# RWKV-7 attention and a hard-swish feed-forward on one core: conversion's steps dealt by a table, and two groups of loads issued later

## The chip, the core and the metric

The kernel runs on one NeuronCore of one Trainium2 chip. The metric is the device time of one launch in microseconds (us); the time before is the median of three runs.

## The reference

Two blocks follow each other. The first is a linear-attention recurrence over 768 steps for 4 batches and 8 heads of 40 features. The second takes its result as 3072 tokens of 320 features through a feed-forward with 2048 hidden features.

```python
for t in range(S):
    y[:, :, t] = einsum('bhd,bhde->bhe', rt, state)
    Sa = einsum('bhde,bhe->bhd', state, at)
    state_decay = state * wt[:, :, None, :] - einsum('bhd,bhe->bhde', Sa, bt)
    state = state_decay + einsum('bhd,bhe->bhde', vt, kt)
x = attn_out.transpose(0, 2, 1, 3).reshape(3072, 320)
h = x @ w_in
out = (h * clip(h + 3, 0, 6) / 6) @ w_out
```

## The kernel before, in words

**Units and groups.** The recurrence is cut in blocks of 64 steps. A unit is one block of two batches (two times 64 steps on the 128 partitions) with all eight heads; there are 24 units, in groups of NU = 4. A unit is first prepared (`prepare`): stage W (turn w, running products), gam (decay factors), A, B and K (turn a, b, k and scale them), F (the 64x64 coupling of a and b), factor (scaled K and B in row form, `KBt`), E (masked scores) and EV (scores times v). Then the triangular coupling of the whole group is inverted (`invert`: 30 pairs of a product and an addition, L661 and L667, one after the other on VectorE), completed by `third_block` (L697 to L730), and each unit takes its step (`step`: RT, VT, C, R, S, U, UT, rS, sn, H, y, then `move` and `move2`, which carry the result to the feed-forward's layout by DMA).

**Feed-forward.** `expand` (L975, with ScalarE L990 and VectorE L991 behind it) and `contract` (L1016) work on tiles of 128 tokens. After the first group they fill the tensor engine beside the later units.

**Conversion of the weights.** The two feed-forward weights arrive as raw 64-bit words and are turned into 32-bit floats in 20 pieces (`load_weights`). A piece of 512 KB is loaded by one to four DMAs (L279) into a temporary home and then takes VectorE's L301, ScalarE's L302 and L304, and VectorE's L321, L325 and L312. `load_weights` is a generator: every `next(weights)` issues one step of it. A home is loaded again only after the piece that was in it is done, and never beyond `limit`.

**What sets the order.** There is no scheduler: every engine and every queue works in the order in which the program emits instructions. The SyncE queue (SP) issues nearly all DMAs, each in its place in that order. Around the change this order has four stretches:

1. `by_twos(0, ...)` prepares units 0 to 3 in turns t = 0 to 13. `fetch` is called inside stages: W fetches the next W, A the next A, factor the next B and K. In `gam_stage` (L503) a unit up to 8 fetches its own v. At t == 0 the first `next(weights)` loads the first two pieces into `tinv` (four DMAs); `limit` then goes to 4 at t == 7 and to 12 at t == 10.
2. `while not third` emits the inversion of the first group. Every third turn, and at a small rate in `by_twos` (MIXED), a step of conversion is put in.
3. `PLAN` emits the steps of units 0 to 3 and the two `third_block` calls (`firsts`, written T). The argument `weight` of `run` puts conversion steps after each pause of a stage: none or 1 in `firsts`, 1.5 on average up to line 6 of the plan, 3 from line 7.
4. At line 8 of the plan the W and A tiles of the second group are allocated and loaded (`seconds`, tile WA). From line 10 the second group's preparation is mixed in, and from there the kernel runs in its steady form.

Of the kernel before, what the change touches and what calls it, by code (L numbers as in the profile page):

```python
# [30 lines left out]
def kernel(  # L31
# [43 lines left out]
    B, H, T, D = r.shape  # L75
# [3 lines left out]
    NU = 2 * NP  # L79
# [107 lines left out]
    for i in range(3):  # L187
        t = const.tile([P, H, BL], F32, name=f"score{i}")
# [14 lines left out]
    for p in range(NP):  # L203
        t = const.tile([P, 2, NPR, SLOT], F32, name=f"state{p}")
        nc.vector.memset(t[:], 0.0)
        state.append(t)
        t = const.tile([P, 2, NPR], F32, name=f"last{p}")
# [175 lines left out]
    def fetch(name, i, engine=None):  # L383

        if i is None or i >= NK:
            return
        x, crossed = {"W": (w, 0), "A": (a, 0), "B": (b, 0), "K": (k, 0), "R": (r, 1),
                      "V": (v, 1)}[name]
        if name == "V":
            t = values[i % AHEAD]  # L390
        else:
            t = (others if i < 2 * NU and i % 2 and name != "R" else inputs)[name]
        g, p = names[i]
        engines = engine or nc.sync
        for q in range(2):
            engine = engines[q] if isinstance(engines, tuple) else engines
            y = x[2 * p + q, :, g * BL:(g + 1) * BL, :]
            rows = slice(q * BL, (q + 1) * BL)
            if crossed:
                for s in range(2):  # L400
                    engine.dma_start(out=t[rows, 4 * s:4 * s + 4, 0:D],  # L401
                                     in_=y[s::2].rearrange("h t e -> t h e"))
            else:
                engine.dma_start(out=t[rows, :, 0:D], in_=y.rearrange("h t e -> t h e"))  # L404
        data[i][name + "N"] = t
# [8 lines left out]
    def turn_pairs(x):  # L414

        o = ps_any([P, NPR, P])
        for n in range(NPR):
            nc.tensor.transpose(out=o[:, n, :],  # L418
                                in_=x[:, 2 * n:2 * n + 2, :].rearrange("p s e -> p (s e)"),
                                identity=ident[:])  # L420
        return o
# [21 lines left out]
    def turned(name):  # L443
        return tmp.tile([P, NPR, P], F32, name=name, tag="turned", bufs=5)
# [24 lines left out]
    def prepare(i, F):  # L469
        n, o = i % NU, data[i]  # L470
# [19 lines left out]
        def gam_stage():  # L490

            gam = o["G"] = grp.tile([P, NPR, P], F32, name="gam", tag="gam", bufs=NU + 2)
            rgam = o["rg"] = tmp.tile([P, NPR, P], F32, name="rgam", bufs=2)
            gv = gam[:].rearrange("p r (q i) -> p (r q) i", q=2)
            rv = rgam[:].rearrange("p r (q i) -> p (r q) i", q=2)
            nc.vector.reciprocal(gv[:, :, 0:HB], o["prods"][:, :, 0, 1:HB + 1][:, :, ::-1])  # L496
            nc.gpsimd.tensor_copy(gv[:, :, HB:BL], o["prods"][:, :, 1, 0:HB])
            nc.gpsimd.tensor_copy(rv[:, :, 0:HB], o["prods"][:, :, 0, 0:HB][:, :, ::-1])
            dec = grp.tile([P, 2, 2, NPR], F32, name="dec", tag="dec", bufs=NU + 2)
            nc.gpsimd.tensor_copy(dec[:].rearrange("p m q r -> p r q m"),  # L500
                                  o["prods"][:].rearrange("p (r q) m i -> p r q m i", q=2)[:, :, :, :, HB])
            o["dec"] = dec
            if i <= 2 * NU:  # L503
                fetch("V", i)
            yield from ()

# [93 lines left out]
        def k_stage():  # L600
            x = turn_pairs(o["KN"])
            yield PE
            kt = o["kt"] = turned("kt")
            nc.vector.tensor_tensor(out=kt[:], in0=x[:], in1=o["rg"][:], op=ALU.mult)

# [24 lines left out]
    def in_turn(stages, order):  # L630

        for name in order:
            yield from stages[name]()
            shared[0] = None
            yield DONE
# [410 lines left out]
    weights = load_weights()  # L1046
    side = deque()
    owed, due = [0.0], [0.0]
# [9 lines left out]
    def aside(n, weight=0):  # L1058

        for _ in range(n):  # L1060
            if side and next(side[0], side) is side:
                side.popleft()
            due[0] += weight
            while due[0] >= 1:
                due[0] -= 1
                next(weights, None)

    def run(stage, steps=0, weight=0, mixed=0):

        for at in stage:  # L1070
            if at == DONE:
                return
            aside(steps, mixed)
            due[0] += weight
            while due[0] >= 1:
                due[0] -= 1
                next(weights, None)

    third, F, group_F = [], None, []

# [11 lines left out]
    RFETCH, EARLY, MIXED = 8, 5, 0.27  # L1092
    TWOS = 14

    def by_twos(first, steps, mixed, rate, fill={}):


        chains = [by_stages(first + i, prepared(first + i)) for i in range(NU)]
        for t in range(TWOS):

            order = [0, 1] if t < STAGES else []
            order += [2, 3] if t > 5 else []
            if t < 2:
                order = [0, 0, 1, 1][4 * t:]
            if t == 3:
                order = [2, 0, 3, 1]
            for i in order:
                run(chains[i], steps if t > 10 else 0, fill.get(t, 0), mixed)
                pieces(rate / 2)
            if t == 10:  # L1110
                side.append(invert(group_F[-1], third, first == 0))
            yield
# [5 lines left out]
        for i in range(2):  # L1118
            fetch(name, i, (nc.sync, nc.scalar) if name == "W" else None)
    for t, _ in enumerate(by_twos(0, 4, MIXED, 0)):  # L1120
        if t == 0:
            next(weights)
        limit[0] = {7: 4, 10: 12}.get(t, limit[0])
        while t == 7 and refill[0]():
            pass
        if t == RFETCH:
            fetch("R", 0)
# [5 lines left out]
    stages = [step(i) for i in range(NU)]  # L1133
    chains = [in_turn(stages[0], ["RT", "VT", "C", "R"]), in_turn(stages[1], ["RT", "VT", "C"])]
    early = deque(chains[i] for i in (0, 0, 1, 1, 0, 1, 0))
    n, cleared = 0, []
    while not third:
        aside(1)
        if not third:
            n += 1  # L1140
            if n % 3 == 1:
                next(weights, None)
            if converted[0] >= 2 and not cleared:
                cleared.append(nc.gpsimd.memset(tinv[:], 0.0))
            if n % EARLY == 0 and early:
                run(early.popleft())
    assert not early and cleared
    limit[0] = 13
    while phase[0] == 1:
        next(weights)  # L1150
    firsts = [third_block(*third[-1], n, True) for n in (0, 2)]
    run(firsts[0])
    run(firsts[0], weight=1)

    def block(i, j):

        if i % NU < 2:
            if j == 0:
# [3 lines left out]

    PLAN = """0 U 0 UT 1 R
              0 sn 0 H T
              1 U 1 UT 0 y
              2 RT T
              1 sn 1 H 2 VT 0 move 0 move2
              1 y 2 R  # L1170
              2 S 3 RT
              1 move 1 move2 2 U 2 UT 2 C
              3 R 3 VT
              2 rS 2 sn 2 H 3 S
              2 y 3 U 3 UT 3 C
              3 rS 3 sn 3 H 2 move
              3 y 2 move2

              3 move
              3 move2"""  # L1180
    PLAN = [deque(line.split()) for line in PLAN.split("\n")]
    BEGIN = 10
    order = [[] for _ in range(NU)]
    plan = []
    for line in PLAN:
        plan.append([])
        while line:
            i = line.popleft()
            if i != "T":
                i = int(i)  # L1190
                order[i].append(line.popleft())
            plan[-1].append(i)
    chains = [in_turn(stages[i], order[i]) for i in range(NU)]
    for t, line in enumerate(plan):
        for i in line:
            if i == "T":
                run(firsts[1])
            else:
                run(chains[i], weight=1.5 if t < 7 else 3)
        if t == 3:  # L1200
            limit[0] = PIECES
        if t == BEGIN - 2:
            seconds()
            for name in "WA":
                fetch(name, NU + 1)
            third.clear()
            second_group = by_twos(NU, 3, 0, 1.25)
        if t == BEGIN + 1:

            for name in "BK":  # L1210
                others[name] = second(name)
                fetch(name, NU + 1)
        if t >= BEGIN - 2:
            pieces(3 if t < BEGIN else 1.5 if t < BEGIN + 3 else 0)
        if t >= BEGIN:
            next(second_group)
# [93 lines left out]
    for i in range(NU, NK):  # L1310
        spread[0] = i >= 2 * NU - 1
        for j in range(BLOCKS):
            rate, inversion = 3.5, 0
            if i + AHEAD >= NK + NU - 1:
                rate = 4.5
            if i < 2 * NU - 1:
                rate = 2.8
            parts = a_block(m)
            next(parts)
            if side or i % NU == NU - 1 and rate < 4:  # L1320

                rate, inversion = 6.2, 2 + (i < 2 * NU)
# [7 lines left out]
            if side:  # L1330
                rate, inversion = 6.2, 2 + (i < 2 * NU)
# [39 lines left out]
```

## Time and profile before

| | |
|---|---|
| median of 3 runs | 824.27 us (823.3 to 826.4) |
| the profiled execution's own time | 823.12 us |
| its span, first to last instruction | 821.4 us |
| granted tensor clock, mean over the span | 0.948 |
| PE busy | 742.0 us, 90% of the span |
| PE busy in 0 to 140 us | 82 us of 140 (sum of the ten-us windows) |
| PE busy in 140 to 820 us | 660.36 us of 680 |
| VectorE (DVE) busy | 534.1 us, 65% |
| ScalarE (ACT) busy | 321.5 us, 39% |
| GpSimd (POOL) busy | 152.4 us, 19% |
| moved by DMA | 45.05 MB, of it 2.05 MB on queue q8 (instructions) |

A timeline line has the start and the length in us, the engine, the source line, the operation, what it writes and reads, how many instructions are merged, and in brackets how long the engine stood idle before it and what ended that. The word "issue" stands where no wait is visible. In the groups of DMA queues, the columns are packets, MB and the share of 16 engines' time.

### The profile page before, as it was taken

How to read it: one execution, taken by the hardware profiler on the slowest of the kernel's cores; microseconds unless marked ns; L12 is line 12 of the kernel's file. 1: busy time of each engine (PE TensorE's matmuls, PEld its weight loads, DVE VectorE, ACT ScalarE, POOL GpSimd, SP SyncE). 2: the span in 40 equal slices, each digit the busy share in tenths (PEclk: the TensorE clock that was granted, in tenths of full speed). 3: DMA queues.
4: the chain of work that ended last, by engine and by line, in shares of the span. 5: the costliest groups of instructions: out<-in, count | busy, mean ns of one | idle time of the engine just before them, and what ended most of it. 6: DMA issues, size and time to landing. Idle time of an engine off the chain costs nothing.

```text
span 821.4 us, 35781 instructions
## 1 busy us (share of the span) xinstructions
PE 742.0 (90%) x15832; PEld 630.1 (77%) x15832; DVE 534.1 (65%) x1090; ACT 321.5 (39%) x847; POOL 152.4 (19%) x297
## 2 busy tenths in 40 slices
PE   4723976989999989999999999999999999999998
PEld 3622866878877878788888888878888888888886
DVE  7799598778855679735699564798546685232210
ACT  1233664222455423544333644334552434332211
POOL 3232101320122130321121222113112102000000
PEclk9855589998999999999999999999999999999999
DMA  6673544331223330332231232132232101110000
GB/s 100 121 181 78 138 119 90 66 59 26 41 50 61 57 63 14 59 53 48 46 59 24 53 66 49 36 57 38 42 61 51 18 22 29 28 21 13 18 19 16
DMA packets 174218, 45.05 MB, mean 55 GB/s; under 512 B 157424, under 2 KB 172784, under 8 KB 174064
## 3 DMA queue, kind: packets, MB, share of 16 engines
q1 hardware_dynamic: 171840, 42.36, 26.8%
q8 instruction: 125, 2.05, 1.0%
q10 hardware_dynamic: 2224, 0.41, 0.3%
q14 instruction: 29, 0.24, 0.1%
HBM read 34.08 MB, written 3.93 MB: 46 GB/s over the span
## 4 chain that ended last, share of the span: by engine, by line
PE 72%; DVE 9%; issue 9%; SPq 3%; DMA 3%; POOL 2%; ACT 2%; DVEq 0%; POOLq 0%; ACTq 0%
PE h L975 24%; PE o L1016 22%; PE any L456 4%; PE any L890 3%; PE any L418 3%; PE any L428 2%; PE any L866 2%; PE any L810 2%; DVE x L667 1%; SPq L401 1%; PE any L771 1%; DVE prod L661 1%; PE any L831 1%; SPq L404 1%; PE any L697 1%
## 5 line engine op out<-in xcount | busy, mean ns | idle before, releaser
L975 PE MATMUL h<-xt,win 128*128 128x128 f32 (+1 forms) x2304 | 251.4, 283 | 9.1 <-DVE gt L991 7.9
L975 PEld LDWEIGHTS h<-xt,win 128*128 128x128 f32 (+1 forms) x2304 | 231.6, 192 | 26.3 <-issue 8.9
L1016 PE MATMUL o<-wout,gt 128*128 128x320 f32 x768 | 230.8, 444 | 0.0
L1016 PEld LDWEIGHTS o<-wout,gt 128*128 128x128 f32 x768 | 138.6, 190 | 50.5 <-issue 0.4
L991 DVE SCALAR_TENSOR_TENSOR gt<-gt,h 128x512 f32<-128x512 f32 x96 | 61.5, 677 | 60.9 <-ACT gt L990 60.9
L990 ACT ACTIVATE gt<-h,three 128x512 f32<-128x512 f32 x96 | 62.2, 686 | 97.5 <-PE h L975 97.2
L875 DVE TENSOR_TENSOR state<-any,state 40x160 f32<-40x160 f32 (+1 forms) x88 | 27.9, 321 | 68.1 <-PE any L866 41.8
L661 DVE TENSOR_TENSOR prod<-x 128x30 f32<-128x30 f32 (+9 forms) x180 | 62.8, 349 | 13.8 <-POOL x L652 8.4
L905 POOL TENSOR_TENSOR yg<-ys,gam 128x512 f32<-128x512 f32 x22 | 39.4, 1789 | 165.7 <-DVE ys L903 110.5
L667 DVE TENSOR_TENSOR x<-x,prod 128x30 f32<-128x30 f32 (+9 forms) x180 | 64.1, 356 | 5.4
L591 POOL TENSOR_TENSOR KBt<-K,rgt 128x320 f32<-128x320 f32 x24 | 21.2, 884 | 246.9 <-ACT rgt L581 225.5
L465 DVE COPY_PREDICATED score<-mask,any 128x256 f32<-128x256 int32 x143 | 53.4, 435 | 6.1 <-PE h L456 3.0
L496 DVE RECIPROCAL gam<-prods 128x256 f32<-128x256 f32 x24 | 41.8, 1748 | 13.6 <-POOL yg L905 13.2
L624 ACT ACTIVATE EV<-any 64x160 f32<-64x160 f32 x92 | 24.8, 296 | 44.3 <-PE any L618 34.8
L511 DVE RECIPROCAL rgam<-prods 128x256 f32<-128x256 f32 x24 | 41.8, 1741 | 0.0
L903 DVE TENSOR_TENSOR ys<-any,ys 128x256 f32<-128x256 f32 x44 | 16.6, 418 | 34.6 <-PE any L618 18.3
L485 DVE TENSOR_TENSOR_SCAN prods<-wm,start 128x528 f32<-128x528 f32 x24 | 30.0, 1251 | 10.7 <-ACT wm L482 8.4
L750 ACT ACTIVATE RT<-any 128x256 f32<-128x256 f32 (+1 forms) x44 | 15.5, 401 | 51.5 <-PE any L428 49.5
L890 PE MATMUL any<-score,KBt 64*64 64x64 f32 x1536 | 31.1, 231 | 1.7 <-DVE state L875 1.7
L890 PEld LDWEIGHTS any<-score,KBt 64*64 64x64 f32 x1536 | 27.3, 144 | 4.5 <-DVE state L875 1.8
L730 ACT ACTIVATE tinv<-any 32x256 f32<-32x256 f32 x48 | 18.0, 375 | 30.3 <-PE any L720 29.7
L776 DVE TENSOR_TENSOR RR<-any,EV 128x160 f32<-128x160 f32 x44 | 12.1, 318 | 25.9 <-PE any L456 25.8
(181 smaller groups left out, 1057.0 us busy)
## 6 DMA issues: line engine op xcount, KB each, us to landing
B<-in_b_dram SPq DMA_DIRECT2D x48, 80.0 KB
K<-in_k_dram SPq DMA_DIRECT2D x48, 80.0 KB
V<-in_v_dram SPq DMA_DIRECT2D x96, 40.0 KB
out_dram<-ob SPq DMA_DIRECT2D x47, 80.0 KB
R<-in_r_dram SPq DMA_DIRECT2D x92, 40.0 KB
A<-in_a_dram SPq DMA_DIRECT2D x40, 80.0 KB
W<-in_w_dram SPq DMA_DIRECT2D x39, 80.0 KB
xt<-yg SPq DMA_DIRECT2D x72, 40.0 KB
```

Source lines behind the costliest of these rows:

```text
L456: nc.tensor.matmul(out=o[i][half(q), n, :], lhsT=lhs[half(i, D), n ^ (2 * q * swap), half(q)], rhs=rhs[half(i, D), n, half(q)], start=True ...
L465: nc.vector.copy_predicated(out=x[:, 4 * i:4 * i + 4, :], mask=mask4, data=o[i])
L496: nc.vector.reciprocal(gv[:, :, 0:HB], o["prods"][:, :, 0, 1:HB + 1][:, :, ::-1])
L511: nc.vector.reciprocal(rv[:, :, HB:BL], o["prods"][:, :, 1, 1:HB + 1])
L661: nc.vector.tensor_tensor(out=pv, in0=_ap(x[:], (i + 1) * L + i, [[L, n], [0, i]]), in1=_ap(x[:], i * L, [[0, n], [1, i]]), op=ALU.mult,)
L667: nc.vector.tensor_tensor(out=rest, in0=rest, in1=pv, op=ALU.add)
L890: nc.tensor.matmul(out=y[q][half(s), pr, :], lhsT=o[name][half(q), h * D:h * D + SLOT], rhs=m[name][half(q), 4 * rs + 2 * s + j, :], start ...
L905: nc.gpsimd.tensor_tensor(out=yg[:], in0=m["ys"][:].rearrange("p r q t -> p r (q t)"), in1=o["G"][:], op=ALU.mult)
L975: nc.tensor.matmul(out=hp[c][:, i, :], lhsT=lhsT, rhs=rhs, start=(begun[c] == 0), stop=(begun[c] == 3 * NQ - 1))
L990: nc.scalar.activation(out=gt[:], in_=hp[c][:], func=AF.Relu, bias=three[:], scale=1.0)
L991: nc.vector.scalar_tensor_tensor(out=gt[:], in0=gt[:], scalar=6.0, in1=hp[c][:], op0=ALU.min, op1=ALU.mult)
L1016: nc.tensor.matmul(out=op[:], lhsT=gts[c][:, n, :], rhs=wout[:, c * HJ + r * NQ + n, :], start=((split or r == 0) and c == 0 and n == 0), ...
```

## The change

Three things are edited.

- **v later.** Units 0 to 3 fetch their v in `k_stage` and no longer in `gam_stage`. Units 4 to 8 fetch theirs where they did.
- **First raw pieces later.** The first `next(weights)` is called at t == 5 and no longer at t == 0.
- **Conversion by a table.** In the inversion a step is put in at the turns listed in `STEPS`. In the plan, `name:n` puts n steps after every pause of that stage; X and Y are the two `third_block` calls. The stages themselves keep their order.

```diff
@@ gam_stage
-            if i <= 2 * NU:
+            if NU <= i <= 2 * NU:
                 fetch("V", i)
@@ k_stage
             yield PE
+            if i < NU:
+                fetch("V", i)
@@
+    def deal(n):
+        for _ in range(n):
+            next(weights, None)
+
-    def run(stage, steps=0, weight=0, mixed=0):
+    def run(stage, steps=0, mixed=0, deals=0):
         for at in stage:
             if at == DONE:
                 return
             aside(steps, mixed)
-            due[0] += weight
-            while due[0] >= 1:
-                due[0] -= 1
-                next(weights, None)
+            deal(deals)
@@ first group
-        if t == 0:
+        if t == 5:
             next(weights)
@@ inversion
+    STEPS = (1, 4, 7, 9, 12, 16, 17, 22, 27, 28, 32, 33, 34, 41, 44, 46, 51, 61, 64)
-            if n % 3 == 1:
+            if n in STEPS:
                 next(weights, None)
@@ plan
-    run(firsts[0])
-    run(firsts[0], weight=1)
-    PLAN = """0 U 0 UT 1 R
-              0 sn 0 H T
-              1 U 1 UT 0 y
-              2 RT T
-              1 sn 1 H 2 VT 0 move 0 move2
-              1 y 2 R
-              2 S 3 RT
-              1 move 1 move2 2 U 2 UT 2 C
-              3 R 3 VT
-              2 rS 2 sn 2 H 3 S
...
+    PLAN = """X X 0U:3 0UT:1 1R
+              0sn:1 0H:2 Y:1
+              1U 1UT:3 0y:2
+              2RT:2 Y
+              1sn 1H:1 2VT:1 0move 0move2
+              1y:2 2R
+              2S:1 3RT
+              1move 1move2 2U:3 2UT:2 2C:4
+              3R:4 3VT:3
+              2rS:3 2sn:3 2H:3 3S:3
...
-                run(chains[i], weight=1.5 if t < 7 else 3)
+            run(chains[name[0]], 0, 0, *map(int, amounts))
```

More of the change, by code (lines that the diff above doesn't have):

```diff
@@ L1093, with by_twos @@
     TWOS = 14
-    def by_twos(first, steps, mixed, rate, fill={}):
+    def by_twos(first, steps, mixed, rate):
         chains = [by_stages(first + i, prepared(first + i)) for i in range(NU)]
@@ L1107, in by_twos @@
             for i in order:
-                run(chains[i], steps if t > 10 else 0, fill.get(t, 0), mixed)
+                run(chains[i], steps if t > 10 else 0, mixed)
                 pieces(rate / 2)
@@ L1161, in block @@
             run(blocks[i])
-    PLAN = """0 U 0 UT 1 R
-              0 sn 0 H T
-              1 U 1 UT 0 y
-              2 RT T
-              1 sn 1 H 2 VT 0 move 0 move2
-              1 y 2 R
-              2 S 3 RT
-              1 move 1 move2 2 U 2 UT 2 C
-              3 R 3 VT
-              2 rS 2 sn 2 H 3 S
[L1175 to L1181, printed above, removed]
-    BEGIN = 10
[L1183 to L1193, printed above, removed]
-    for t, line in enumerate(plan):
[L1195 to L1198, printed above, removed]
-                run(chains[i], weight=1.5 if t < 7 else 3)
+    PLAN = """X X 0U:3 0UT:1 1R
[8 more added lines that the diff above has]
+              2rS:3 2sn:3 2H:3 3S:3
+              2y:3 3U:4 3UT:2 3C:5
+              3rS:3 3sn:3 3H:3 2move
+              3y:1 2move2
+              3move
+              3move2"""
+    BEGIN = 10
+    plan = [[x.split(":") for x in line.split()] for line in PLAN.split("\n")]
+    chains = {str(i): in_turn(stages[i], [x[0][1:] for line in plan for x in line if x[0][0] == str(i)])
+              for i in range(NU)}
+    chains.update({x: firsts[n] for n, x in enumerate("XY")})
+    for t, line in enumerate(plan):
+        for name, *amounts in line:
+            run(chains[name[0]], 0, 0, *map(int, amounts))
         if t == 3:
```

## The prediction

> **What bounds the kernel now.** I read the page's forty slices first, then the chain that ended last, then the timelines of SP, PE, DVE and ACT for the first 150 us, and last the DMA queues in one-us windows. From 140 us PE is busy 660.36 of 680 us in an order that the change leaves alone, so the end is set by when the dense part begins. In the first 140 us it is busy about 82. So a microsecond won before 140 moves the end by about one.
>
> The start is a queue of DMA issues. SP's timeline:
>
> ```profile
> 10.53 1.27 SPq L404 DMA_DIRECT2D W<-in_w_dram  x2
> 11.84 2.61 SPq L401 DMA_DIRECT2D V<-in_v_dram  x4
> 14.55 1.27 SPq L404 DMA_DIRECT2D WA<-in_w_dram  x2
> 15.87 2.62 SPq L401 DMA_DIRECT2D V<-in_v_dram  x4
> 18.53 2.00 SPq L279 DMA_DIRECT2D tinv<-in_moe_w_in_dram  x4
> 20.63 1.29 SPq L404 DMA_DIRECT2D A<-in_a_dram  x2
> ```
>
> SP issues without a pause, 0.65 us for each DMA, and unit 3's w (WA) stands behind unit 0's v. PE and DVE show who waits:
>
> ```profile
> 18.26 1.09 PE L418 MATMUL h<-ident,WA 128*128 128x128 f32 x4 [2.17 <-DMA WA<-in_w_dram]
> 29.14 0.36 PE L456 MATMUL any<-at,kt 40*64 40x64 f32 x1 [3.38 <-issue]
> 20.13 1.26 DVE L485 TENSOR_TENSOR_SCAN prods<-wm,start 128x528 f32<-128x528 f32 x1 [1.94 <-issue]
> 30.10 0.44 DVE L465 COPY_PREDICATED score<-mask,any 128x256 f32<-128x256 int32 x1 [3.04 <-PE h L456]
> ```
>
> From 30.10 DVE works on with no idle before the transpose that opens the inversion but 1.09 us (38.74), and from 42.28 to 77 it is full. The second stall, in the midst of unit 1's scores E, has no visible releaser. The DMA queues in the windows 23 to 24 and 26 to 27 us show one:
>
> ```profile
> q1 hardware_dynamic: 73, 0.24, 100.9%
> q8 instruction: 1, 0.02, 9.4%
> ```
>
> The raw weights fill all 16 engines[...]. The other place that matters lies later:
>
> ```profile
> 122.12 0.43 DVE L301 TENSOR_SCALAR parts<-raw_fb 128x512 uint32<-128x512 uint32 x1 [0.46 <-DMA raw_fb<-in_moe_w_out_dram]
> 124.44 1.26 ACT L990 ACTIVATE gt<-h,three 128x512 f32<-128x512 f32 x2
> 125.89 2.08 PE L975 MATMUL h<-xt,win 128*128 128x128 f32 x8 [4.30 <-DVE gt L991]
> 143.94 1.49 PE L890 MATMUL any<-score,KBt 64*64 64x64 f32 x62 [1.66 <-DVE state L875]
> ```
>
> PE waits for gt, gt for ACT's conversion steps ahead of it (122.58 to 124.06), these for piece 17's load. The last line is the hand-over: DVE, full from 130 to 145, releases PE into the dense part.
>
> [...] q8 has 125 packets in 2.05 MB. PE stalls at about its 216th matmul and again at about the 466th (1.17 us before 40.37)[...]. The trace has clock 0.50 from 44 to 102 us and again around 110 to 114.
>
> **The change, part by part** (times in the frame of the trace before).
>
> *v and raw pieces leave the front of SP.* Four DMAs go from ahead of unit 3's w: it is issued at 11.84, 2.7 us earlier. Unit 2's w took 2.3 us from the end of its issue to PE's start, so unit 3's is there at about 15.5, before PE has finished B at 15.9. PE loses its 2.17 us wait and shifts by 2.36. DVE's second scan then waits only for ACT's copies, which wait for the scan before (ends 17.60): 18.45 in place of 20.13, a gain of 1.7; unit 0's mask ends at 25.4.
>
> *The refill.* [...] In flight then are v, W and A, no raw piece: SP reaches those only after B and K of units 2 and 3, whose tiles GpSimd frees at 22.8 and 24.5, so B and K go from 22.8 to 28.0 and the raw pieces at 28.0. [...] PE goes on at 25.2, its scores end at 26.15. DVE's mask moves from 30.10 to 26.15: **3.95 us**. Ends: [...] 4.7 if PE never stalls, since DVE itself comes at 25.4.
>
> *What follows it.* A and B of units 2 and 3 must be turned by 28 and 31: landed by about 18 and 29. The next places on DVE (7.6 us of work) shift whole; the inversion starts 3.9 us earlier. Work that was hidden: the first piece's L301 at 38.5 needs a load issued at 28 to 29; 512 KB at the 0.24 MB per us of that window lands by about 33, cover 5 us. V of units 2 and 3 now stand behind two more raw pieces and R, and land about 45; PE needs the last at 46.3, and what is queued behind it, R's transposes, feeds an ACT copy that stood until 58.08 behind conversion: cover about 6 us. [...] Cost of all three: nothing, and one for one beyond the cover.
>
> *STEPS.* DVE has the same 20 conversion instructions in the inversion, each moved by at most two places; DVE is full there, so the sum is unchanged: 0.
>
> *The plan.* Two ACT instructions (0.72 each) go from ahead of `tinv` (L730, 81.72) to behind it; the second ended at 81.69, the matmuls before at 81.3, so **0.3 us**. Between 104 and 113 a pair moves behind S and RT, so PE's waits for S, U and UT (1.54, 1.49, 0.96) shrink by some 2 us together. But DVE is full from 99 to 118 with the same instructions, and the next is a load. Piece 16 goes on SP from behind piece 15 to behind R and unit 1's eight moves: from 107 to about 117. Piece 17 goes behind the four WA loads: from 117.42 to about 121.3. With 4.7 us to land, as piece 17 took, DVE gets piece 16 at about 121.5 (it came at 119.04) and waits 3 us, and piece 17 at 126. In return gt needs only piece 16 and stands ahead of piece 17 on ACT and DVE: ACT at 123.9 for 124.44. After y, piece 19's L301 comes at 132.5 to 133 for 133.12. I take **0.5 us**; ends −3 (each of the last four loads a microsecond later than assumed) and +2.6 (SP's 2.03 us stall in R, which follows two raw pieces, goes, and piece 16 lands in 3 us).
>
> Sum: 3.9 + 0.3 + 0.5 = 4.7 us, against the profiled execution's 823.12 (span 821.4): 818.4. The median of the runs is 1.15 higher; 824.27 − 4.7 = **819.6**.
>
> **Rivals.** *Only the w wait goes*: [...] Gain 2.4 + 0.3 = 2.7, 821.6. *The late pieces take it back*: −3 in the plan, gain 1.2, 823.1. For it: DVE already waited for pieces 17 and 18 (0.46, 0.47). *Both ends are kind*: 4.7 + 0.3 + 2.6 = 7.6, 816.7. For it: PE's 4.0 us of waits for ACT at 104 to 113 are shortened. *Slower: the clock returns later.* It came back at 102 after 18 us of work at half rate[...]. If the shifted work misses it until 122, the 10.2 busy us of PE from 102 to 122 double; 10.2 − 4.7 makes 5.5 us more, 829.8. It decides from about 110 on. Against it: PE's order is unchanged and its gaps shrink. A change without effect is excluded by SP's order alone.
>
> **How the numbers follow.** The forecast has 0.48 (own range 818 to 821, of it 0.38 under the bound), the kind case 0.15, only-w 0.20, late pieces 0.09, the clock 0.08. 0.5%, 4.1 us, is about what a measurement of this kernel can tell from no change: faster below 820.15. Faster 0.53, same 0.39, slower 0.08. The range 816.0 to 824.0 takes in all but the clock and the tails.
>
> **What would show it.** Right: unit 3's w turned by PE before 16.5, no 3 us stall in E, unit 1's mask at about 26, the transpose before the inversion at about 35; the same 35 us of inversion; L991 before piece 17's L301. Wrong: a DVE wait for `tinv`'s load at the first L301, PE waiting for v for over 6 us, waits on pieces 16 to 18 of over 3 us in sum beyond those counted, or half clock after 110.

## The result, and the profile after

| | before | after |
|---|---|---|
| median of 11 runs each | 823.68 us | 821.54 us |
| ratio after to before, 95% interval | | 0.9979 [0.9961, 0.9996] |
| the profiled execution's own time | 823.12 us | 820.82 us |
| its span | 821.4 us | 819.1 us |
| granted tensor clock, mean | 0.948 | 0.948 |

The kernel is about 2 us faster. 4.7 were forecast. The lead was won at the start, and about half of the 3 us with which the inversion opened was given back by 136 us.

**The start.** First SP's timeline of the kernel after (start, length, engine, line, operation, output and input, instructions merged):

```profile
11.89 1.27 SPq L404 DMA_DIRECT2D WA<-in_w_dram  x2
...
17.33 6.15 SPq L401 DMA_DIRECT2D V<-in_v_dram  x8
23.59 1.27 SPq L404 DMA_DIRECT2D B<-in_b_dram  x2
...
26.33 1.28 SPq L404 DMA_DIRECT2D B<-in_b_dram  x2
...
29.58 2.02 SPq L279 DMA_DIRECT2D tinv<-in_moe_w_in_dram  x4
```

Unit 3's w (WA) now follows unit 2's at once (11.89, where it was 14.55), and the first raw pieces (`tinv`) stand last. But all eight DMAs for v stand just ahead of the B tiles of units 2 and 3. PE's and then DVE's timeline of the same kernel show what that brings:

```profile
15.93 1.06 PE L418 MATMUL h<-ident,WA 128*128 128x128 f32 x4
...
17.53 1.04 PE L418 MATMUL any<-ident,K 128*128 128x128 f32 x8
...
23.13 0.27 PE L456 MATMUL any<-at,kt 40*64 40x64 f32 x1 [0.92 <-issue]
...
30.41 0.63 PE L418 MATMUL h<-ident,B 128*128 128x128 f32 x4 [2.43 <-DMA B<-in_b_dram]
...
31.90 1.09 PE L418 MATMUL any<-ident,K 128*128 128x128 f32 x4
```

```profile
18.68 1.26 DVE L485 TENSOR_TENSOR_SCAN prods<-wm,start 128x528 f32<-128x528 f32 x1 [0.26 <-issue]
...
24.90 1.04 DVE L465 COPY_PREDICATED score<-mask,any 128x256 f32<-128x256 int32 x3
...
33.02 0.69 DVE L606 TENSOR_TENSOR kt<-any,rgam 128x512 f32<-128x512 f32 x1 [0.55 <-PE any L418]
35.68 2.12 DVE L651 STREAM_TRANSPOSE fb<-F 128x1024 f32<-128x1024 f32 x1 [1.96 <-ACT F L542]
```

In the kernel before, the turns of K and the transpose that opens the inversion stood here (PE and DVE):

```profile
19.99 1.92 PE L418 MATMUL any<-ident,K 128*128 128x128 f32 x8
38.74 2.11 DVE L649 STREAM_TRANSPOSE fb<-F 128x1024 f32<-128x1024 f32 x1 [1.09 <-ACT F L542]
```

The wait for w is gone, and the turns behind it took less time. The stall in unit 1's scores E shrank from 3.38 to 0.92 us. Unit 1's mask, the third instruction of the row at 24.90, ran at about 25.6 where it was 30.10: 4.5 us earlier. Ten us later the lead was 3.06, since DVE stood 0.55 and 1.96 us (1.09 before): unit 3's B, issued at 26.33, reached PE only at 30.41. The DMA queues show an instruction packet. In the window 20 to 21 us of the kernel after:

```profile
q1 hardware_dynamic: 378, 0.06, 50.2%
q8 instruction: 1, 0.02, 8.1%
```

The engines are half busy with v. In the kernel before, 54.5% were busy in the packet's own window (26 to 27), but they had been full from 22 to 26 (99.6, 100.9, 112.9 and 139.1% in q1's four windows). In both kernels the window of the packet begins 3.1 us before PE goes on: at 26 for 29.14 and at 20 for 23.13. I took the stall for a wait for instructions and call it the refill. The view doesn't name the engine that the packet is for, so the refill is inferred, not shown.

**The plan.** SP's timeline of the kernel after, later on:

```profile
103.02 0.52 SPq L279 DMA_DIRECT2D raw<-in_moe_w_out_dram  x1
103.64 3.57 SPq L401 DMA_DIRECT2D R<-in_r_dram  x4
...
113.75 0.53 SPq L279 DMA_DIRECT2D raw<-in_moe_w_out_dram  x1
114.37 1.36 SPq L404 DMA_DIRECT2D WA<-in_w_dram  x2
...
117.20 0.57 SPq L279 DMA_DIRECT2D raw_fb<-in_moe_w_out_dram  x1
```

Piece 15 goes at 103.02, piece 16 at 113.75 behind R and unit 1's moves, piece 17 at 117.20 behind WA. In the kernel before, SP's timeline had pieces 15 and 16 together, and piece 17 ahead of WA:

```profile
106.42 1.07 SPq L279 DMA_DIRECT2D raw<-in_moe_w_out_dram  x2
...
117.42 0.54 SPq L279 DMA_DIRECT2D raw_fb<-in_moe_w_out_dram  x1
```

DVE's timeline of the kernel after (L301 is the first instruction of a piece):

```profile
118.07 0.43 DVE L301 TENSOR_SCALAR parts<-raw 128x512 uint32<-128x512 uint32 x1 [2.86 <-DMA raw<-in_moe_w_out_dram]
...
121.10 1.29 DVE L993 SCALAR_TENSOR_TENSOR gt<-gt,h 128x512 f32<-128x512 f32 x2 [0.27 <-ACT gt L992]
123.57 0.43 DVE L301 TENSOR_SCALAR parts<-raw_fb 128x512 uint32<-128x512 uint32 x1 [1.18 <-DMA raw_fb<-in_moe_w_out_dram]
...
135.11 1.26 DVE L485 TENSOR_TENSOR_SCAN prods<-wm,start 128x528 f32<-128x528 f32 x1 [1.31 <-ACT wm L482]
```

The last wait is new: the first scan of unit 4 waits for ACT's copy of w. In the kernel before, neither that scan nor PE's scores C of unit 3 waited (DVE and PE):

```profile
136.58 1.25 DVE L485 TENSOR_TENSOR_SCAN prods<-wm,start 128x528 f32<-128x528 f32 x1
130.65 0.68 PE L456 MATMUL any<-RT,VT 40*64 40x64 f32 x30
```

ACT's and PE's timelines of the kernel after show why:

```profile
120.39 1.26 ACT L992 ACTIVATE gt<-h,three 128x512 f32<-128x512 f32 x2
...
128.68 0.72 ACT L302 ACTIVATE parts<-parts,low 128x512 f32<-128x512 int32 x1 [3.17 <-DVE parts L301]
...
130.06 0.48 ACT L817 ACTIVATE U<-any 128x160 f32<-128x160 f32 x2
```

```profile
121.84 2.08 PE L977 MATMUL h<-xt,win 128*128 128x128 f32 x8 [5.68 <-DVE gt L993]
...
130.40 1.12 PE L456 MATMUL any<-RT,VT 40*64 40x64 f32 x30 [3.10 <-ACT U L817]
...
133.32 1.06 PE L418 MATMUL any<-ident,W 128*128 128x128 f32 x4
...
142.47 1.50 PE L892 MATMUL any<-score,KBt 64*64 64x64 f32 x64
```

Unit 3's U stands on ACT behind the two steps of piece 18, which wait for DVE. PE waits 3.10 us for it, goes on at half clock (four turns of w take 1.06 us at a granted clock of 0.50; 0.60 at 1.00 in the kernel before), and w comes late. The hand-over, taken as the row of y's matmuls from which PE waits no more, is at 142.47, 1.47 us earlier than before.

The lead of after over before, in the two traces:

| place | before | after | lead |
|---|---|---|---|
| unit 1's mask E (DVE) | 30.10 | 25.6 | 4.5 |
| transpose that opens the inversion | 38.74 | 35.68 | 3.06 |
| transpose that closes it | 75.45 | 73.02 | 2.43 |
| piece 15's L301 | 115.66 | 112.66 | 3.00 |
| piece 16's L301 | 119.04 | 118.07 | 0.97 |
| `gt` (DVE) | 125.15 | 121.10 | 4.05 |
| piece 19's L301 | 133.12 | 130.23 | 2.89 |
| scan of unit 4 | 136.58 | 135.11 | 1.47 |
| hand-over (PE, y of unit 3) | 143.94 | 142.47 | 1.47 |
| end | 821.4 | 819.1 | 2.3 |

From hand-over to end are 677.46 us before and 676.63 after. Over all fourteen profiled kernels of this study it is 674.6 to 677.9, so a single trace tells a lead to about 2 us and the timed ratios decide.

### The profile page after: what moved, and what is told of

It reads as the page before. It is cut to its first block, busy times and chain, and to the rows that moved or that the text cites. A ratio compares the mean times of both kernels' runs of the same rounds, so it can differ in the third digit from the quotient of the medians.

```text
span 819.1 us, 35789 instructions
## 1 busy us (share of the span) xinstructions
PE 742.1 (91%) x15832; PEld 630.1 (77%) x15832; DVE 534.2 (65%) x1090; ACT 321.1 (39%) x847; POOL 152.4 (19%) x297
## 4 chain that ended last, share of the span: by engine, by line
PE 71%; issue 9%; DVE 8%; DMA 5%; SPq 3%; POOL 2%; ACT 1%; DVEq 0%; POOLq 0%; ACTq 0%
PE h L977 24%; PE o L1018 22%; PE any L456 4%; PE any L892 3%; PE any L418 3%; PE any L868 2%; PE any L428 2%; SPq L404 2%; PE any L812 1%; DVE x L669 1%; DVE prod L663 1%; PE any L773 1%; PE any L849 1%; PE any L833 1%; SPq L401 1%
## 5 line engine op out<-in xcount | busy, mean ns | idle before, releaser
L1018 PEld LDWEIGHTS o<-wout,gt 128*128 128x128 f32 x768 | 138.7, 190 | 50.5 <-issue 0.4
L778 DVE TENSOR_TENSOR RR<-any,EV 128x160 f32<-128x160 f32 x44 | 12.2, 318 | 25.6 <-PE any L456 25.5
```

Of the source, the lines that this page charges most:

```text
L1018: nc.tensor.matmul(out=op[:], lhsT=gts[c][:, n, :], rhs=wout[:, c * HJ + r * NQ + n, :], start=((split or r == 0) and c == 0 and n == 0), ...
```

## The experiments

Twelve kernels were timed in three groups of four, in the order of the table, 6 to 22 runs each. Every group was on another chip and is compared with runs of the kernel before on that chip, so kernels of one group compare best.

| kernel | median | before in its group | ratio, 95% interval |
|---|---|---|---|
| fetches alone | 820.36 | 823.43 | 0.9961 [0.9947, 0.9976] |
| table alone | 824.16 | 823.43 | 1.0013 [0.9997, 1.0029] |
| change, U free | 820.87 | 823.43 | 0.9971 [0.9957, 0.9986] |
| change, U free, loads early | 816.28 | 823.43 | 0.9907 [0.9891, 0.9924] |
| change, loads early | 815.87 | 823.01 | 0.9922 [0.9904, 0.9940] |
| table alone, U free, loads early | 818.68 | 823.01 | 0.9954 [0.9936, 0.9971] |
| v alone | 824.35 | 823.01 | 1.0014 [0.9999, 1.0028] |
| raw pieces alone | 820.06 | 823.01 | 0.9964 [0.9949, 0.9979] |
| change, piece 16 early | 818.36 | 822.77 | 0.9944 [0.9929, 0.9959] |
| change, piece 17 early | 821.04 | 822.77 | 0.9985 [0.9972, 0.9997] |
| change, loads early, v where it was | 818.21 | 822.77 | 0.9946 [0.9926, 0.9967] |
| change, loads early, B ahead of K | 817.27 | 822.77 | 0.9935 [0.9912, 0.9958] |

Two theories for the lost gain were stated. **A:** the new order on ACT holds U, so PE, w and unit 4's scan are late. **B:** the last loads of raw weights hold the hand-over.

### Half of the change at a time

Fetches alone: the kernel before with the two edits of the start.

```diff
-            if i <= 2 * NU:
+            if NU <= i <= 2 * NU:
                 fetch("V", i)
@@ k_stage, after its pause
+            if i < NU:
+                fetch("V", i)
@@ first group
-        if t == 0:
+        if t == 5:
             next(weights)
```

> The kernel before with the two moved groups of loads alone, its dealing of conversion as it was. Theory A (the moved loads win about 3 us at the inversion; the table gives part of it back at unit 3's U, which the new order puts behind piece 18's conversion on ScalarE): 2.4 to 3.2 us faster than before, the lead of about 2.5 at the inversion's end kept through the last conversion and at the hand-over into the dense part. Theory B (whatever the order, the last loads of raw weights hold the hand-over, so an early start is lost there): no more than 1.5 us faster, VectorE waiting longer for pieces 16 to 19 than before.

Measured: 3.1 us faster, 0.9961 [0.9947, 0.9976]. The inversion's transpose stands at 35.17, and DVE has no wait for any of the pieces 16 to 19. That is A's case; B as it was put there, whatever the order, fell. What is called B from here on is narrower: the table's own order issues pieces 16 and 17 too late.

Table alone: the changed kernel with these three edits taken back.

> The kernel before with the new dealing alone, the loads of v and of the first raw pieces where they were. Theory A: the inversion starts at 42.3 as before, unit 3's U comes about 1 to 3 us later than in the kernel before, and the time is 0 to 1.5 us above before. Theory B: VectorE waits for piece 16 (some 3 us), the time is 1 to 3 us above before. Were the table itself a gain, as the prediction's 0.8 us for it had it: 0.5 to 1 us below before.

Measured: 1.0013 [0.9997, 1.0029], so no gain and rather a loss of about 1 us. DVE's timeline of the table alone:

```profile
119.82 0.43 DVE L301 TENSOR_SCALAR parts<-raw 128x512 uint32<-128x512 uint32 x1 [1.34 <-DMA raw<-in_moe_w_out_dram]
...
125.65 0.43 DVE L301 TENSOR_SCALAR parts<-raw_fb 128x512 uint32<-128x512 uint32 x1 [1.51 <-DMA raw_fb<-in_moe_w_out_dram]
...
136.66 1.26 DVE L485 TENSOR_TENSOR_SCAN prods<-wm,start 128x528 f32<-128x528 f32 x1 [1.31 <-ACT wm L482]
```

The same three waits as in the whole change, so this run doesn't part A from B. The halves add up: 3.1 less 0.7 is 2.4 by the medians, and the whole measured 2.1. So the start gave most of what I had asked of it. The table, which I had put at a gain of 0.8 (0.3 and 0.5), shows none; it measures a cost of about 0.7 to 1, which the interval doesn't part from nothing.

### Which part of the table costs: U or the loads

U free: the six steps between U and UT are put behind unit 3's C, all else as changed.

```diff
-              2y:3 3U:4 3UT:2 3C:5
+              2y:3 3U 3UT 3C:11
```

> The changed kernel with one line of its plan redealt: no conversion steps in unit 3's U and UT, all eleven behind its C, so that ScalarE copies U and UT before the steps of pieces 18 and 19; VectorE's order is untouched. Theory A: the 3.1 us wait of the tensor engine for U goes to under 0.5, its clock stays full over the next w transpose, VectorE's scan follows unit 3's mask without the 1.31 us wait; 1 to 2 us faster than the changed kernel, 3 to 4 below before. Theory B: less than 0.5 us faster than the changed kernel.

Measured: 0.9971 [0.9957, 0.9986]; the changed kernel has 0.9979 [0.9961, 0.9996]. PE's wait for U and the scan's wait are gone from the trace, and PE keeps its full rate there (four turns of w in 0.60 us, 1.06 in the change). But DVE still waits 3.15 us for piece 16 and 1.02 for piece 17, and PE 5.57 us for gt. And PE, no longer held at U, stands later instead: 0.76, 1.10 and 0.94 us between 136 and 143. Theory A is at best a small part.

U free and loads early: pieces 16 and 17 are issued where the kernel before issued them.

```diff
-              2S:1 3RT
+              2S:1 3RT:2
-              3R:4 3VT:3
-              2rS:3 2sn:3 2H:3 3S:3
-              2y:3 3U:4 3UT:2 3C:5
+              3R:4 3VT:4
+              2rS:2 2sn:2 2H:2 3S:3
+              2y:3 3U 3UT 3C:11
```

> As the one with U free, and besides two conversion steps more ahead of unit 3's R load and one more in its VT, three fewer in the next line, so that pieces 16 and 17 are issued where the kernel before issued them, while gt stays ahead of piece 17's conversion. VectorE's waits for pieces 16 and 17 (2.86 and 1.18 us in the changed kernel) should shrink to under 1 in sum. Theory B: this wins 2 to 3 us over the kernel with U free. Theory A: 1 us or less over it, if what waits behind VectorE is bound by the tensor engine by then. In both 3.5 to 6 us below before.

Measured: 0.9907 [0.9891, 0.9924], 7.2 us faster than before and 4.6 faster than with U free alone: more than either case had. SP's timeline of this kernel:

```profile
104.66 1.07 SPq L279 DMA_DIRECT2D raw<-in_moe_w_out_dram  x2
...
115.07 0.53 SPq L279 DMA_DIRECT2D raw_fb<-in_moe_w_out_dram  x1
```

Pieces 15 and 16 now go together at 104.66. DVE's timeline of the same kernel:

```profile
114.67 0.42 DVE L301 TENSOR_SCALAR parts<-raw 128x512 uint32<-128x512 uint32 x1
118.60 1.28 DVE L993 SCALAR_TENSOR_TENSOR gt<-gt,h 128x512 f32<-128x512 f32 x2 [0.86 <-ACT gt L992]
119.81 0.42 DVE L301 TENSOR_SCALAR parts<-raw_fb 128x512 uint32<-128x512 uint32 x1
```

No wait for 16 and 17; piece 18 now is the one that DVE waits for (1.80 us at 124.80). gt stands ahead of piece 17's conversion as in the change, so against the kernel with U free the order is kept and only the loads have moved. PE's wait for gt falls from 5.68 to 1.50 us, and its next eight matmuls take 1.16 us in place of 2.08.

Loads early with U where the change has it: the same but for the last line of the plan, `2y:3 3U:4 3UT:2 3C:5`.

> The changed kernel with pieces 16 and 17 issued where the kernel before issued them, as in the run before (815 to 817 us), but with the plan's own counts 3U:4 3UT:2 3C:5, so that PE again waits for unit 3's U behind piece 18's two steps on ACT. Late loads alone hold the hand-over: within 1 us of the run with both edits, ratio 0.990 to 0.992. The place of U matters once the loads are early: about 2 to 3 us slower than that run (PE's wait of 3.1 us and 0.7 us more at half clock come back), ratio 0.994, and a wait of over 2 us before the scores C of unit 3.

Measured: 0.9922 [0.9904, 0.9940], 7.1 us by the medians: the first case. PE's and DVE's timelines of this kernel:

```profile
125.38 1.13 PE L456 MATMUL any<-RT,VT 40*64 40x64 f32 x30 [4.26 <-ACT U L817]
```

```profile
130.10 1.26 DVE L485 TENSOR_TENSOR_SCAN prods<-wm,start 128x528 f32<-128x528 f32 x1 [1.32 <-ACT wm L482]
```

The wait for U is longer than in the change (3.10), and the scan still stands 1.32 us. Without U's wait the ratio is 0.0015 lower here and 0.0008 lower with late loads, or 1.2 and 0.7 us; each is within the intervals, so these runs don't part it from nothing. With the loads early the same kernel goes from 0.9979 to 0.9922, and these intervals lie apart. So the late loads hold the hand-over.

The stretch of DVE from piece 15's L301 to unit 3's mask C, read from the traces of these kernels and of before, says the same. With late loads it lasts 20.37 (change), 18.64 (table alone) and 21.37 us (U free); with early loads 17.28 (U free) and 17.39; on the old plan 20.26 (before) and 19.57 (fetches alone).

The table with a free U and early loads on the old start:

> The table with early loads and a free U as in the 816.3 us kernel, but on the old start: v and the raw pieces fetched where the kernel before fetches them. If the start's lead (3.1 us, measured alone) and the plan's gain add up: about 819.5 us, ratio 0.995. If early loads only pay because the start gives them room: no faster than the kernel before, 823 us or more. The trace of the first case shows no wait for piece 16 and gt before piece 17's L301.

Measured: 0.9954 [0.9936, 0.9971], 4.3 us faster; the first case. 4.3 and the start's 3.1 make 7.4, close to the 7.2 of both. So the table's order with early loads and a free U is good by itself and needs no lead from the start. What spoiled it was the place of two loads. Why it is good was not tested alone: the traces fit gt, which no longer stands behind a later piece (ACT's part of it at 120.09 here, 124.44 before; PE waits 1.55 us for it, 4.30 before), but no run moves gt by itself.

### One load at a time

Piece 16 early, piece 17 still behind WA:

```diff
-              2S:1 3RT
+              2S:1 3RT:2
-              3R:4 3VT:3
+              3R:4 3VT:1
```

> The changed kernel with piece 16 alone issued early (behind piece 15, ahead of R and of unit 1's moves); piece 17 stays behind the WA loads. If the lateness of piece 16 is what held gt and the hand-over: its wait of 2.86 us goes and the run comes within 1.5 us of the one with both early (815.9), ratio 0.991 to 0.994. If piece 17 or the sum of both decides: 819 to 821, ratio 0.995 to 0.9975, with DVE waiting 2 to 4 us for piece 17 instead.

Measured: 0.9944 [0.9929, 0.9959], between the two cases. The wait moved: DVE's timeline of this kernel has

```profile
126.07 0.43 DVE L301 TENSOR_SCALAR parts<-raw_fb 128x512 uint32<-128x512 uint32 x1 [2.31 <-DMA raw_fb<-in_moe_w_out_dram]
```

for piece 17 and no wait for piece 16, and PE's wait for gt fell from 5.68 to 1.95 us. Piece 17 early, piece 16 still late:

```diff
-              3R:4 3VT:3
-              2rS:3 2sn:3 2H:3 3S:3
+              3R:4 3VT:5
+              2rS:2 2sn:2 2H:2 3S:3
```

> The changed kernel with piece 17 alone issued early (ahead of the WA loads); piece 16 stays behind R and unit 1's moves. If piece 16 decides: as the changed kernel, its wait of about 3 us stays, ratio 0.9965 to 0.998. If piece 17 decides: near the run with both early, ratio 0.991 to 0.994.

Measured: 0.9985 [0.9972, 0.9997], as the changed kernel, so close to the first case by its time. DVE's wait for piece 16 is not the forecast 3 us but 0.94, with 1.67 more for ACT's part of gt. So piece 16 first: early by itself it brings about 2.9 us over the change (0.0035). Piece 17 beside it would be about 1.8 more (to 0.9922), but there the intervals overlap. Alone, piece 17 shows no gain.

### What gave the start its gain

v alone and raw pieces alone, each on the kernel before. First v:

> The kernel before with v alone fetched in k_stage; the raw pieces stay at t == 0, now right behind unit 3's w (issued from about 13.3). By my reading of the start the wait for w (2.17 us) goes and the refill in unit 1's scores E still meets raw data: a stall of 2 to 3 us, unit 1's mask 1.5 to 2.5 us earlier than 30.10, ratio 0.998. If raw data is not what delays the refill, the stall falls to about 1 us all the same, the mask comes 4 us earlier and the ratio is 0.996 as with both.

Measured: 1.0014 [0.9999, 1.0028]; no gain. Both cases missed it. PE's timeline of this kernel:

```profile
23.74 0.27 PE L456 MATMUL any<-at,kt 40*64 40x64 f32 x1 [1.72 <-issue]
...
29.48 0.79 PE L620 MATMUL any<-V,score 64*64 64x40 f32 x30 [1.98 <-DMA V<-in_v_dram]
31.84 1.09 PE L418 MATMUL h<-ident,B 128*128 128x128 f32 x4 [1.57 <-DMA B<-in_b_dram]
...
34.77 1.09 PE L418 MATMUL h<-ident,B 128*128 128x128 f32 x4 [1.84 <-DMA B<-in_b_dram]
```

The wait for w is gone, the stall in E halved (1.72 us, 3.38 before), unit 1's mask came at about 25.4. All of that was lost within ten us: PE then waited for v, for unit 2's B and for unit 3's B, and the inversion's transpose stood at 40.12, 1.4 us later than before. SP's timeline of this kernel has the reason:

```profile
21.03 6.30 SPq L401 DMA_DIRECT2D V<-in_v_dram  x8
27.44 1.90 SPq L404 DMA_DIRECT2D B<-in_b_dram  x2
```

Eight DMAs, of which four stood ahead of unit 3's w, stand ahead of B instead. The queue is no shorter. Then the raw pieces:

> The kernel before with the first raw pieces alone moved to t == 5; v stays in gam_stage and so ahead of unit 3's w. By my reading PE keeps its wait of about 2.2 us for w and DVE its second scan at about 20.1, but the stall in E falls from 3.4 to about 1 us: unit 1's mask 2 to 2.5 us earlier, ratio 0.9975. If the wait for w is the whole of it: no gain, ratio 1.000.

Measured: 0.9964 [0.9949, 0.9979], the first case and as much as both moves (0.9961). PE's timeline of this kernel:

```profile
18.19 1.09 PE L418 MATMUL h<-ident,WA 128*128 128x128 f32 x4 [2.33 <-DMA WA<-in_w_dram]
26.89 0.36 PE L456 MATMUL any<-at,kt 40*64 40x64 f32 x1 [1.22 <-issue]
```

The wait for w is all there, the stall fell from 3.38 to 1.22, B is issued at 24.98 and 27.73 (26.93 and 30.46 before), PE waits for neither, and the inversion opens at 36.81. Moving the raw pieces gave the start its gain, to within the intervals. The run does not part what they did to the stall from what they did to B, since one move of 1 MB changed both.

Both loads early, with v left where the kernel before fetches it:

> Both pieces early as in the 815.9 us kernel, but v left in gam_stage: of the start only the first raw pieces are moved. If v's move is worth nothing, as the two single runs of the start say: as that kernel, ratio 0.991 to 0.994, with PE still waiting about 2.2 us for unit 3's w. If v's move helps beside the raw pieces': 1 to 2 us slower, ratio 0.994 or more.

Measured: 0.9946 [0.9926, 0.9967]; with v moved, 0.9922 [0.9904, 0.9940] in another group. The value falls on the second case's side of the border, but the intervals overlap, so whether v's move is worth up to 2 us beside the raw pieces' stays open. The trace has 2.45 us of wait for w, 1.68 of stall, and the inversion at 36.19.

B ahead of K: in `factor_stage` unit 0 fetches B alone, unit 1 fetches its B and then both K.

```diff
-            for name in "BK":
-                fetch(name, following(i))
+            for name, j in {0: [("B", 0)], 1: [("B", 1), ("K", 0), ("K", 1)]}.get(i, [("B", i), ("K", i)]):
+                fetch(name, following(j))
```

> The 815.9 us kernel (both pieces early) with the B tiles of units 2 and 3 issued one behind the other, ahead of the two K tiles; so unit 3's B goes about 1.4 us earlier. If its landing is what took back the lead between unit 1's mask and the inversion (1.4 us in the changed kernel): PE's wait for B shrinks by 1 to 1.4 us and the time by up to 1 us, 815 us, ratio 0.991. If K of unit 2 becomes what is late: PE waits for it instead and nothing changes, ratio 0.992.

Measured: 0.9935 [0.9912, 0.9958], no better than without (0.9922 in another group). The second case: PE's timeline of this kernel has

```profile
29.06 1.09 PE L418 MATMUL h<-ident,B 128*128 128x128 f32 x4 [0.38 <-DMA B<-in_b_dram]
31.13 2.13 PE L418 MATMUL any<-ident,K 128*128 128x128 f32 x8 [0.98 <-DMA K<-in_k_dram]
```

With U free and loads early, on the same start without this edit, PE waits 1.06 us for unit 3's B and 0.67 for K; the wait went from B to K. The two kernels with both loads early and the change's own start are the fastest that were run: 816.28 us (0.9907) and 815.87 us (0.9922).

## Why the prediction was right or wrong

**What bounds the kernel: right.** The hand-over near 140 us and the end moved together to within the 2 us named above. In the four kernels with both loads early and the raw pieces moved, the hand-over lies between 137.3 and 138.7, and they are 4.6 to 7.2 us faster than before by the medians.

**w earlier: right on the wait, wrong on its worth.** w was turned at 15.93, the scan stood at 18.68 (18.45 forecast). In *only the w wait goes* I gave that wait 2.4 us. The raw-alone run keeps it and gains as much as both moves, within the intervals; the v-alone run removes it and gains nothing. It was an earlier link in a chain whose next one, B of units 2 and 3, was late for its own reason.

**The stall in E (the refill): right in direction, and its number partly by luck.** Unit 1's mask was forecast at 26.15 and came at about 25.6, but not by the sum. PE went on at 23.13, where I had 25.2, and DVE did not wait for it at all: it came to the mask when DVE itself was free, the outer case of 25.4. Two terms were off. I let PE's work shift by 2.36 us; but behind the w wait its turns also took less time (eight of K 1.04 us where they had taken 1.92), and the products of F began at 19.37, 4.1 us earlier. And the length that I gave the stall rested on an assumed way of fetching instructions, which no trace shows; the stall itself was 0.92. The kernel before stalls 3.38 us, and the nine others whose PE timeline was read here 0.86 to 1.74. Five of those nine have the start of the change, and their stalls range from 0.86 to 1.68, so differences of a us between single traces mean nothing. PE then stands 1.99 us at 38.87 in after (2.92 with the fetches alone, 3.22 with the raw pieces alone), while DVE is in the inversion and does not wait. In two other kernels the profile puts that pause down to DVE's transpose (1.22 us with piece 16 early, 1.77 with B ahead of K), so its cause is open.

**"The next places on DVE shift whole": the first step that came out short.** I had B of unit 3 landed by about 29. PE got it at 30.41, and 4.5 us of lead became 3.06. B's landing is not all of it: behind this pause PE's granted clock fell, from 1.00 at 30 to 31 us to 0.50 at 32 to 36 (1.00 at 34 to 42 before), so K and F took longer (four turns of K 1.09 us at 31.90, eight 1.09 at 35.32 before), and DVE's wait for F grew to 1.96 us. In the change with loads early, whose start is the same, DVE did not wait for PE's turns of K (0.55 us in after), waited 1.23 us for F, and the transpose stood at 34.05. In the six other kernels with both moves of the start and B and K in the change's order, the opening transpose lies between 34.05 and 36.66, mean 35.3: 2.1 to 4.7 us ahead, mean 3.4. So 3.9 lay inside the spread and above its middle. By time the start gave 3.1 (2.0 to 4.4 by the interval).

**STEPS at 0: small, but not nothing.** From the opening to the closing transpose the old steps take 36.71 us (before) and 36.98 to 37.02 (fetches, v or raw pieces alone); the table's take 37.10 and 37.07 on the old start, and 37.30 to 37.34 on the new. So STEPS costs about 0.35 and the new fetches 0.3: the 0.63 us that after lost there.

**The plan: the step that failed, by sign.** I forecast a gain of 0.5 and 0.3; the table alone measures a cost of about 1 (1.0013 [0.9997, 1.0029]). The 0.3 at `tinv` is not what failed: the lead grew from 2.43 at the closing transpose to 3.00 at piece 15. The 0.5 is. I had seen the late issue and DVE's 3 us for piece 16 (2.86), and let gt's earlier place make up for them. The runs show that it doesn't: the same kernel with the two loads early is 4.7 us faster (0.9979 to 0.9922), so their lateness costs more than the table's order wins.

Taking 3.9 off my places gives piece 16 at 117.6 (118.07 measured), ACT's gt at 120.0 (120.39), piece 17 at 122.1 (123.57), piece 19 at 128.6 to 129.1 (130.23). Two terms were off. I let piece 17 land 4.7 us after its issue, as before; it took 6.4, and DVE stood 1.18 us for it. Pieces 18 and 19 now follow it within 2.6 us on SP (117.87 and 119.79; 122.03 and 122.69 before), which may be why, but no run shows it. And I stopped at piece 19: the next link is the scan of unit 4, which needs w, which needs PE past C of unit 3, which needs U from ACT. I had booked the moved pairs as shorter waits of PE for U at 104 to 113 and did not ask where on ACT unit 3's U would stand: 3.10 us of PE's wait and 1.31 us of the scan's. U's order alone could not be shown as a gain in time, so only the loads are established.

**The rivals.** *The late pieces take it back* named the right mechanism and put it at −3 us; it was about −1 against before, and about 5 against what the same table gives with early loads. *The clock returns later* did not come: the clock was full again at 100 us (102 before), and for a while already from 90 to 92. But two short losses of the same kind lie on the path, after the waits of 5.68 and 3.10 us; the first has its like in before, after 4.30 us. Pauses of 3.10 (after) and 3.34 us (table alone) were followed by half rate: four turns of w took 1.06 us behind each. The length of a pause alone does not tell it: behind one of 1.64 us (U free, loads early, at 23.84) the four turns of unit 3's a took 1.06 us, behind one of 1.68 (fetches alone, at 24.83) 0.60. Behind the 3.10 us in after, half clock lasted 6.5 us of nearly gapless work, from 130.4 to about 137.

## What to carry to other kernels

When a load is dealt to another place, follow it on the queue first: two weight pieces issued 8.5 and 2.1 us later (113.75 and 117.20 in after, about 105.2 and 115.07 with U free and loads early) cost all that the better order of arithmetic gained. With them put back and U free, a table that lost about 1 us won 4. Moving transfers away from one waiting tile puts them ahead of another, so the value of a freed wait is what remains at the next tile's landing; taking the bulk data out of the queue left the wait for w (2.33 us) but shortened the stall in E (3.38 to 1.22) and freed B behind it. And follow the chain up to the hand-over itself, not to the last item that was moved: here ACT's order behind it held one more wait, 3.10 us of PE for U and 1.31 us of DVE's scan for w.

## What the runs showed of the hardware that was not expected

PE stalled at the same place in unit 1's scores, behind the 217th matmul, in all ten kernels whose PE timeline was read there: for 3.38 us in the kernel before, which issues 1 MB of raw weights at 18.53 us, and for 0.86 to 1.74 us in the nine with a changed start. The table alone, and the same table with U free and loads early, keep the old start; there DVE's mask waits 1.95 and 2.20 us for PE's scores (3.04 before). In before and in after an instruction packet stands in a window that begins 3.1 us before PE goes on.

Piece 16, 512 KB as one DMA, was used 4.3 us after its issue (113.75 to 118.07) and piece 17 took longer (117.20 to 123.57, both waited for). Before, piece 16 was issued at about 107.0 and used without a wait at 119.04. So a later place on SP turned a hidden load into a wait.

The time for which PE stays at half clock after a pause varied at nearly gapless work. In after it was 6.5 us from the pause's end: windows of 2 us have the granted clock at 0.51, 0.50, 0.50 and 0.78 from 130 to 138. With B ahead of K, turns of w took 1.06 us at 129.53 and 0.60 at 131.63, after a pause of 3.83 us that ended at 127.05: at most 4.6 us. There the first matmuls behind the pause still ran at full rate (30 in 0.69 us at 127.05), as in after behind the pause that ended at 30.41 (four turns of B in 0.63 us). What sets either was not tried.
